# A first layer in plain float32: reordering the lead-in of a chunked attention and mixture-of-experts kernel

## The chip, the cores and the metric

The kernel runs on one core of a Trainium2 chip. The metric is device time in microseconds (us) of one launch. A launch has one program; the inputs are laid out on the host before it (heads split, w1's rows reordered), no arithmetic is done there.

## The reference

Two stages, all float32. Inputs: r, k, v, w of shape (4 batches, 8 heads, 768 positions, 48), u (8, 48), expert weights w1 (4, 384, 1024), w2 (4, 1024, 384) and probabilities for 3072 rows and 4 experts.

```python
for t in range(S):                      # per batch and head, state is 48x48
    cur = einsum('bhd,bhe->bhde', u * k[t], v[t])
    y[t] = einsum('bhd,bhde->bhe', r[t], state + cur)
    state = w[t][..., None] * state + einsum('bhd,bhe->bhde', k[t], v[t])
x = y as rows of 384                    # 8 heads x 48
p = domain_probs / (domain_probs.sum(-1) + 1e-9)
out = sum over e of p[:, e] * (relu(x @ w1[e]) @ w2[e])
```

## The kernel before

**Units and passes.** The 768 positions are cut into 6 chunks of 128; a chunk of one batch is a unit (n = 4 * chunk + batch, 24 units). The experts' part works on blocks; block c is chunk c of all four batches, 512 rows. Passes are pairs of a group of blocks, (0), (1, 2), (3, 4, 5), and an expert; pass 0 is block 0 with expert 0. A turn is one block in one pass: first layer `f1` for 8 tiles of 128 hidden columns, then second layer `f2` per batch. In pass 0 the turn is cut in two half turns of two batches each (`SEG = (2, 2)`), so that the first can start when units 0 and 1 are done.

**Split products.** A float32 matrix is split in a high part (rounded to float32r) and a low part (the rest), and a product is three float32r matmuls: high x high, high x low, low x high. `split_w` makes the parts of a quarter of w1 or w2: one cast on ScalarE, two subtractions of half a tile each on GpSimd (or VectorE). In `f1` a tile takes 9 matmuls (3 slices of the 384 inputs by 3 products), in `f2` 24 per batch. The activation's parts are `hh` (ScalarE) and `hl` (VectorE).

**A unit.** `after_decays` and `until_decays` are scans of the decays on VectorE, `scale` multiplies r and k by them (VectorE), `own_product` and `own_score` make the diagonal term (GpSimd, VectorE's reduction `dg`, then two tiles `a`, one for each head of a pair, from ident on GpSimd or ScalarE), `scores` are plain float32 matmuls of k with r and transposes of k, `masking` copies the scores into `a` (VectorE), `values` multiplies v with `a`, `carry` makes the state. `guard` checks the decays in place (three ScalarE instructions). Four head pairs come out of `values`; x has three slices of 128 rows, each with two heads of 48 rows in rows 0 to 47 and 64 to 111, and the last pair's 96 values are spread over the 2 x 16 rows that are free in each slice. `fill` does that spreading with two DMAs per unit from the tile `y3` (for chunk 0), after ScalarE and VectorE split the values.

**Order.** The order of every engine's work is the order in which the program is written; each engine runs its own instructions in that order, and SP issues all loads in one order too. Up to pass 0 the order is written out by hand (lines 496 to 558). Then `turn` calls `between` after each f1 tile and each quarter of an f2 block (16 calls a half turn), and `gap` adds a pace to a credit and runs one attention step (`go`) per whole credit: `step_a` (after_decays of n+1, scores of n, loads, own_product), `step_b` (until_decays), `step_c` (masking), `step_d` (scale, own_score), `step_e` (values, carry, fill, guard, loads). `work` puts the weight splits in: w2 of a fresh expert in the first half turn, w1 of the next pass in the last second layer. Weights come through a ring `raw` of 4 tiles; `warm_up` issues float32r matmuls on zeros.

Of the kernel before, what the change touches and what calls it, by code (L numbers as in the profile page):

```python
# [20 lines left out]
C = 128  # L21
# [20 lines left out]


@with_exitstack
def chunked_path(ctx, tc, dmaj, tmaj, u_bc, probs, w1, w2, out, flag):
# [35 lines left out]

    def half(j):
        return slice(64 * j, 64 * j + D)
# [26 lines left out]
    def setup_b():  # L110
        nc.gpsimd.memset(mid, -W_MID)
        nc.gpsimd.memset(edge, -W_HALF * W_HALF)
        for t in sd:
            nc.gpsimd.memset(t, 0.0)

# [7 lines left out]
    raw_t, wt = {}, {}  # L123

# [22 lines left out]
    un, xb = {}, {}  # L147
    NU = B * NCH

    def load(n, what):  # L150
# [11 lines left out]
        elif what == "own":  # L162
            if n == 1:

                t = p_acc.tile([128, B, DM], F32, name="acc", tag="acc").rearrange("p b d -> p (b d)")
            else:
                t = p_one.tile([128, 2 * DM], F32, name="rkt", tag="rkt")
            nc.sync.dma_start(out=t[:, 0:2 * DM], in_=tmaj[n, :, 0:2 * DM])
# [11 lines left out]
    def own_score(n):  # L180
# [5 lines left out]
        for q in range(2):  # L186
            a = p_two.tile([128, NP, C], F32, name=f"a{q}", tag=f"a{q}")
            if n <= SEG[0] and q == 1:
# [64 lines left out]
    def values(n):  # L253
        s = un[n]
        c, b, v = s["c"], s["b"], s["v"]

        yp = ps_sc.tile([128, 2, NP, C], F32, name="yp", tag="sc")
        if c == 0:
            y = yp.rearrange("p g (i z) t -> p (g i) z t", z=2)[:, :, 0, :]
        else:  # L260


            y = [yp[:, i % 2, i // 2, :] for i in range(NP)]
            for i in range(NP):
                for j in range(2):
                    o = j ^ (i % 2)
                    nc.tensor.matmul(y[i][wide(o)], sd[n % 2][half(j), i * D:i * D + (64 if o == 0 else D)],  # L267
                                     s["rr"][half(j), i, :], start=(i < 2), stop=False, skip_group_check=True)
        for i in range(NP):
            for j in range(2):  # L270
                h = 2 * i + j
                if c == 0:
                    nc.tensor.matmul(y[wide(j), i, :], v[:, h * D:h * D + (64 if j == 0 else D)],  # L273
                                     s["a"][j][:, i, :], start=(i % 2 == 0), stop=(i % 2 == 1),
                                     skip_group_check=True)
                else:
                    nc.tensor.matmul(y[i][half(j ^ (i % 2))], v[:, h * D:(h + 1) * D], s["a"][j][:, i, :],  # L277
                                     start=False, stop=(i >= 2), skip_group_check=True)
        if c not in xb:
            xb[c] = p_x.tile([128, KT, B, 2, C], F32R, name="x", tag="x")  # L280
        x = xb[c]
        y3 = s["y3"] = p_two.tile([ROWS, 2, 2, C], F32R, name="y3", tag="y3")

        for dst, src in places(s, y if c == 0 else yp):
            nc.scalar.copy(dst[:, :, 0], src)
        for dst, src in places(s, y if c == 0 else yp):
            nc.vector.tensor_tensor(dst[:, :, 1], src, dst[:, :, 0].bitcast(F32), ALU.subtract)

    def places(s, y):
        x, y3 = xb[s["c"]][0:ROWS, :, s["b"]], s["y3"]  # L290
        if s["c"] == 0:
            return (y3[:, 1:2], y[0:ROWS, 3:4]), (x, y[0:ROWS, 0:3])
        return (y3, y[0:ROWS, 1, 0:2]), (x[:, 0::2], y[0:ROWS, 0, 0:2])

    def fill(n):

        s = un[n]
        x, y3 = xb[s["c"]], s["y3"]
        for j in range(2):
            o = 1 - j if s["c"] > 0 else j  # L300
            nc.sync.dma_start(out=x[64 * j + D:64 * (j + 1), :, s["b"]].bitcast(F32),
                              in_=y3[half(o), 1].bitcast(F32))
            if s["c"] > 0:
                nc.sync.dma_start(out=x[half(j), 1, s["b"]].bitcast(F32), in_=y3[half(o), 0].bitcast(F32))
# [39 lines left out]
    def f1(e, blk, f, t0=0, nt=B * C):  # L344
        q, o = divmod(f, FT // NQ)
        wh, wl = wt[e, 1, q]
# [3 lines left out]
        for k in range(KT):  # L350
            for n, (wv, i) in enumerate(((wh, 0), (wh, 1), (wl, 0))):
                nc.tensor.matmul(p[:, 0:nt], wv[:, k, fs], x[:, k, bs, i, :],  # L352
                                 start=(k == 0 and n == 0), stop=(k == KT - 1 and n == 2))
# [80 lines left out]
    steps = [(f, n) for n in range(NU) for f in parts]  # L434
    steps += [(None, NU - 1)] * 8 + [(step_f, NU - 1)]
# [20 lines left out]
    rawq = [(passes[i][1], which, q) for i in fresh for which in (1, 2) for q in range(NQ)]  # L456
# [24 lines left out]
    def turn(e, blk, first, last, b0, nb, work):  # L481
# [3 lines left out]
        def between():  # L485
            work(done[0])
            gap(done[0])
            done[0] += 1

        for f in range(FT):  # L490
            f1(e, blk, f, b0 * C, nb * C)
# [4 lines left out]
    with tc.manual_schedule():  # L496
# [7 lines left out]
        for what in ("w", "k", "r", "own", "v"):  # L504
            load(1, what)
        nc.sync.dma_start(out=pr, in_=probs)
        for q in range(NQ):
            more_raw()
        setup_b()

        decays(0)
        scale(0)
        own_product(0)
        own_score(0)
        after_decays(1)
        scores(0)
        masking(0)
        load(2, "k")
        load(2, "r")
        load(2, "own")  # L520
        guard(0)
        load(2, "w")
        own_product(1)
        until_decays(1)
        scale(1)
        warm_up(FILL[1])
        values(0)
        carry(0)
        fill(0)
        own_score(1)  # L530
        load(2, "v")
        scores(1)
        split_w((0, 1, 0), True)
        masking(1)
        after_decays(2)
        own_product(2)
        warm_up(FILL[2])
        values(1)
        carry(1)
        fill(1)  # L540
        split_w((0, 1, 1), True)
        guard(1)
        setup_c()
        until_decays(2)
        split_w((0, 1, 2), True)
# [230 lines left out]
```

## Time and profile before

| | us |
|---|---|
| median of 3 runs | 930.29 |
| the runs | 930.41, 930.29, 928.63 |
| profiled execution | 928.05 |
| its span, first to last instruction | 926.3 |
| TensorE (PE) busy | 901.4 (97%) |
| VectorE (DVE) / ScalarE (ACT) / GpSimd (POOL) busy | 359.6 / 254.7 / 279.1 |

The chain that ended last is 94% TensorE (44% the second layer, 42% the first layer). PE is the matmuls, PEld the weight loads, SP the engine that issues DMAs; L352 is line 352. "Granted clock" is the share of TensorE's full clock, 1.0 for 2.4 GHz and 0.5 for 1.2 GHz. Busy times of engines overlap, so only TensorE's says something about the span here. The first fortieths of the span are the only ones in which TensorE is not nine tenths busy or more, besides the last.

### The profile page before, as it was taken

Reading aid. Unit: us, or ns where it says so; the run is one execution under the profiler, and the core shown is the slowest. Engines: PE = TensorE matmul, PEld = TensorE weight load, DVE = VectorE, ACT = ScalarE, POOL = GpSimd, SP = SyncE. Lnnn points to the kernel's source line nnn. Section 1 sums busy time; section 2 is a strip of 40 time slices with the busy share of each in tenths; the row PEclk is TensorE's granted clock in tenths of the full one; section 3 lists DMA queues with packets and bytes.
Section 4 is the critical chain, followed back from the end, with each engine's and each line's share of the span. In section 5 each row is a group of like instructions: output and inputs, shape, how many; then the busy total and the mean of one; then the engine's idle time right before and its main releaser. Section 6 shows DMA issues by size and latency. Waiting matters only on the chain.

```text
span 926.3 us, 13725 instructions
## 1 busy us (share of the span) xinstructions
PE 901.4 (97%) x5617; PEld 811.2 (88%) x5617; DVE 359.6 (39%) x567; ACT 254.7 (27%) x462; POOL 279.1 (30%) x283
## 2 busy tenths in 40 slices
PE   7689999999999999999999999999999999999996
PEld 5679889898988989989989898899899899889986
DVE  7756465555454452222455643102222222221221
ACT  3534434313234322231221322232202310321120
POOL 3845667531145414214213220033003300230000
PEclk7789999999999999999999999999999999999999
DMA  8543545432234322102323220022002200111001
GB/s 249 182 129 105 163 149 158 152 105 73 65 115 119 123 72 73 65 1 85 100 81 114 80 79 12 24 69 69 1 1 69 69 1 1 32 37 35 17 18 39
DMA packets 37097, 72.47 MB, mean 78 GB/s; under 512 B 5152, under 2 KB 15648, under 8 KB 37024
## 3 DMA queue, kind: packets, MB, share of 16 engines
q1 hardware_dynamic: 37024, 71.49, 25.2%
q8 instruction: 46, 0.75, 0.3%
q14 instruction: 27, 0.22, 0.1%
HBM read 62.43 MB, written 4.72 MB: 72 GB/s over the span
## 4 chain that ended last, share of the span: by engine, by line
PE 94%; DVE 2%; DMA 2%; ACT 1%; issue 1%; SPq 0%; DVEq 0%
PE pf L372 44%; PE pf L352 42%; PE sc L235 3%; PE yp L277 2%; PE yp L267 1%; PE kt L241 1%; PE up L315 1%; DMA k<-in_dmaj 1%; DMA raw<-in_w 1%; PE yp L273 0%; DVE w2l L142 0%; DMA x<-y 0%; DVE k L227 0%; DVE e L216 0%; PE pf L108 0%
## 5 line engine op out<-in xcount | busy, mean ns | idle before, releaser
L352 PE MATMUL pf<-x,w1h 128*128 128x512 f32 (+1 forms) x1200 | 365.0, 387 | 9.5 <-DMA x<-y 7.0
L352 PEld LDWEIGHTS pf<-x,w1h 128*128 128x128 f32 x1200 | 224.6, 192 | 52.5 <-issue 4.4
L372 PE MATMUL pf<-w2h,hh 128*128 128x384 f32 x768 | 259.3, 338 | 0.0
L372 PE MATMUL pf<-w2h,hl 128*128 128x384 f32 x768 | 257.1, 335 | 0.0
L372 PE MATMUL pf<-w2l,hh 128*128 128x384 f32 x768 | 256.8, 334 | 0.0
L359 DVE SCALAR_TENSOR_TENSOR hl<-pf,hh 128x512 fp32r<-128x512 f32 (+1 forms) x200 | 133.7, 669 | 287.3 <-ACT hh L358 286.9
L358 ACT ACTIVATE hh<-pf 128x512 fp32r<-128x512 f32 (+1 forms) x200 | 116.3, 581 | 448.5 <-PE pf L352 448.4
L352 PE MATMUL pf<-x,w1l 128*128 128x512 f32 (+1 forms) x600 | 231.2, 385 | 0.0
L142 POOL TENSOR_TENSOR w1l<-raw,w1h 128x384 fp32r<-128x384 f32 x80 | 85.1, 1092 | 255.4 <-ACT w1h L137 243.9
L372 PEld LDWEIGHTS pf<-w2h,hh 128*128 128x128 f32 x768 | 144.2, 188 | 2.2 <-issue 0.6
L372 PEld LDWEIGHTS pf<-w2l,hh 128*128 128x128 f32 x768 | 144.2, 188 | 0.8
L372 PEld LDWEIGHTS pf<-w2h,hl 128*128 128x128 f32 x768 | 144.2, 188 | 0.0
L352 PEld LDWEIGHTS pf<-x,w1l 128*128 128x128 f32 x600 | 115.1, 192 | 21.8
L381 DVE SCALAR_TENSOR_TENSOR acc<-pf,pr,acc 128x384 f32<-128x384 f32 x72 | 44.5, 618 | 202.9 <-PE pf L372 202.8
L142 POOL TENSOR_TENSOR w2l<-raw,w2h 128x384 fp32r<-128x384 f32 x78 | 82.6, 1080 | 106.7 <-ACT w2h L137 100.8
L192 POOL TENSOR_TENSOR a<-ident,dg 128x512 f32<-128x512 f32 x45 | 47.7, 1080 | 153.6 <-DVE dg L184 153.6
L235 PEld LDWEIGHTS sc<-r,k 48*128 48x128 f32 x384 | 25.2, 199 | 13.1 <-issue 9.3
L235 PE MATMUL sc<-r,k 48*128 48x128 f32 x384 | 30.0, 299 | 6.2 <-DVE k L227 4.2
L216 DVE TENSOR_TENSOR_SCAN e<-wx,zst 112x516 f32<-112x516 f32 x24 | 34.4, 1433 | 0.8
L251 DVE COPY_PREDICATED a<-mask,sc 128x512 f32<-128x512 uint32 x48 | 32.1, 723 | 3.4 <-POOL a L192 2.1
L379 ACT ACTIVATE acc<-pf,pr 128x384 f32<-128x384 f32 x24 | 14.0, 582 | 70.3 <-PE pf L372 70.2
L204 DVE TENSOR_TENSOR_SCAN g<-wx,ones 112x516 f32<-112x516 f32 x24 | 32.0, 1335 | 2.9 <-DMA wx<-in_dmaj 2.9
(67 smaller groups left out, 436.0 us busy)
## 6 DMA issues: line engine op xcount, KB each, us to landing
raw<-in_w SPq DMA_DIRECT2D x80, 384.0 KB, 3.2
rkt<-in_tmaj SPq DMA_DIRECT2D x23, 384.0 KB, 3.1
wx<-in_dmaj SPq DMA_DIRECT2D x24, 226.2 KB, 3.0
k<-in_dmaj SPq DMA_DIRECT2D x24, 224.0 KB, 3.8
r<-in_dmaj SPq DMA_DIRECT2D x24, 224.0 KB, 3.5
v<-in_tmaj SPq DMA_DIRECT2D x24, 192.0 KB, 2.9
out<-acc SPq DMA_DIRECT2D x24, 192.0 KB, 1.9
x<-y SPq DMA_DIRECT2D x88, 48.0 KB, 2.2
```

The costliest lines, as they stand in the source:

```text
L142: eng.tensor_tensor(lo[:, s], t[:, s], hi[:, s].bitcast(F32), ALU.subtract)
L192: nc.gpsimd.tensor_tensor(a, ident.unsqueeze(1).to_broadcast([128, NP, C]), dg[:, q].unsqueeze(2).to_broadcast([128, NP, C]), ALU.mult)
L204: nc.vector.tensor_tensor_scan(g[:, WLEN - 1:0:-1], wx[:, WLEN - 1:0:-1], ones1[:, WLEN - 1:0:-1], 0.0, ALU.mult, ALU.add)
L216: nc.vector.tensor_tensor_scan(e, wx[:, 0:WLEN - 1], zst.rearrange("p i t -> p (i t)"), 0.0, ALU.mult, ALU.add)
L235: nc.tensor.matmul(sc[:, j, i, :], s["kk"][half(j), i, :], s["rr"][half(j), i, :], start=True, stop=True)
L251: nc.vector.copy_predicated(s["a"][j], mask.unsqueeze(1).to_broadcast([128, NP, C]), s["sc"][:, j])
L277: nc.tensor.matmul(y[i][half(j ^ (i % 2))], v[:, h * D:(h + 1) * D], s["a"][j][:, i, :], start=False, stop=(i >= 2), skip_group_check=True)
L352: nc.tensor.matmul(p[:, 0:nt], wv[:, k, fs], x[:, k, bs, i, :], start=(k == 0 and n == 0), stop=(k == KT - 1 and n == 2))
L358: nc.scalar.activation(hh[:, ts], p[:, 0:nt], AF.Relu)
L359: nc.vector.scalar_tensor_tensor(hl[:, ts], p[:, 0:nt], 0.0, hh[:, ts].bitcast(F32), ALU.max, ALU.subtract)
L372: nc.tensor.matmul(p, hv[:, ts], wv[:, o, :], start=(f == 0 and n == 0), stop=(f == FT - 1 and n == 2))
L381: nc.vector.scalar_tensor_tensor(a[:, b, :], p, sc, a[:, b, :], ALU.mult, ALU.add)
```

## The change

- In pass 0, `f1` multiplies x and w1 in plain float32 (`plain`): 3 matmul calls a tile in place of 9. w1 of expert 0 is loaded unsplit into `w1_own`, which takes one buffer of the x pool, and x unsplit into `x_own`, which takes a buffer of the acc pool. `split_x` makes the float32r parts of x later, in the second layer of pass 0, for the other passes.
- For chunk 0 `values` accumulates all in one tile of the f1 pool: for each of the three slices, two matmuls with the weights `vz`, zeros in 48 of 64 columns and the last pair's v in the other 16 (copied by GpSimd in `last_pair`), and two with v. One ScalarE copy writes x. `fill` does nothing for chunk 0.
- Loads, guards and splits are reordered in the part that is written by hand; unit 1's two diagonal tiles are both made by ScalarE; the fourth warm-up is not called; unit 3's steps go a, c, b, e, d; the first half turn's attention steps are listed in `script`; the pace of the second half turn is (0.2, 0.6).

```diff
FILL = (12, 4, 4, 4)
+DIAG = {0: "pa", 1: "aa", 2: "pa"}
...
     zero = const.tile([128, B * C], F32R, name="zero")
+    vz = [const.tile([128, 2, KT, 64], F32, name=f"vz{i}") for i in range(2)]
...
             nc.gpsimd.memset(t, 0.0)
+        for t in vz:
+            nc.gpsimd.memset(t, 0.0)
...
     raw_t, wt = {}, {}
+    w1_own = p_x.tile([128, NQ, KT * FQ], F32R, name="x", tag="x").bitcast(F32)
+    def load_own(q):
+        nc.sync.dma_start(out=w1_own[:, q], in_=w1[0, q])
...
         wt[key] = (hi.rearrange("p (a f) -> p a f", a=a), lo.rearrange("p (a f) -> p a f", a=a))
-    un, xb = {}, {}
+    un, xb, spare = {}, {}, []
...
             if n == 1:
-                t = p_acc.tile([128, B, DM], F32, name="acc", tag="acc").rearrange("p b d -> p (b d)")
+                spare.append(p_acc.tile([128, B, DM], F32, name="acc", tag="acc").rearrange("p b d -> p (b d)"))
+            if n in (1, 3):
+                t = spare[0][:, (n - 1) * DM:(n + 1) * DM]
...
                 t = p_one.tile([128, 2 * DM], F32, name="rkt", tag="rkt")
-            nc.sync.dma_start(out=t[:, 0:2 * DM], in_=tmaj[n, :, 0:2 * DM])
+            nc.sync.dma_start(out=t, in_=tmaj[n, :, 0:2 * DM])
...
             a = p_two.tile([128, NP, C], F32, name=f"a{q}", tag=f"a{q}")
-            if n <= SEG[0] and q == 1:
+            if DIAG.get(n, "pp")[q] == "a":
...
         c, b, v = s["c"], s["b"], s["v"]
+        if c not in xb:
+            xb[c] = p_x.tile([128, KT, B, 2, C], F32R, name="x", tag="x")
+        x = xb[c]
+        if c == 0:
+            y = ps_f1.tile([128, B * C], F32, name="pf1", tag="pf1")[:, 0:KT * C].rearrange("p (i t) -> p i t", i=KT)
+            z = vz[n % 2]
+            for i in range(KT):
+                for j in range(2):
+                    nc.tensor.matmul(y[64 * j:64 * (j + 1), i, :], z[:, j, i, :], s["a"][j][:, KT, :],
+                                     start=(i == 0), stop=False, skip_group_check=True)
+                for j in range(2):
+                    h = 2 * i + j
+                    nc.tensor.matmul(y[half(j), i, :], v[:, h * D:(h + 1) * D], s["a"][j][:, i, :],
+                                     start=False, stop=(i == KT - 1), skip_group_check=True)
+            nc.scalar.copy(x_own()[:, :, b], y)
+            return
         yp = ps_sc.tile([128, 2, NP, C], F32, name="yp", tag="sc")
...
+    def last_pair(n):
+        v = un[n]["v"][:, 2 * KT * D:].rearrange("p (j g k) -> p j k g", j=2, k=KT)
+        nc.gpsimd.tensor_copy(vz[n % 2][:, :, :, D:], v)
+    def x_own():
+        if len(spare) < 2:
+            spare.append(p_acc.tile([128, B, DM], F32, name="acc", tag="acc").rearrange("p b d -> p (b d)"))
+        return spare[1].rearrange("p (k b t) -> p k b t", k=KT, b=B)
+    def split_x(b):
+        x, t = xb[0][:, :, b], x_own()[:, :, b]
+        nc.scalar.copy(x[:, :, 0], t)
+        nc.vector.tensor_tensor(x[:, :, 1], t, x[:, :, 0].bitcast(F32), ALU.subtract)
+    def fill(n):
+        s = un[n]
         if s["c"] == 0:
+            return
...
-    def f1(e, blk, f, t0=0, nt=B * C):
+    def f1(e, blk, f, t0, nt, plain):
         q, o = divmod(f, FT // NQ)
-        wh, wl = wt[e, 1, q]
...
         p = ps_f1.tile([128, B * C], F32, name="pf1", tag="pf1")
-        for k in range(KT):
-            for n, (wv, i) in enumerate(((wh, 0), (wh, 1), (wl, 0))):
-                nc.tensor.matmul(p[:, 0:nt], wv[:, k, fs], x[:, k, bs, i, :],
-                                 start=(k == 0 and n == 0), stop=(k == KT - 1 and n == 2))
+        if plain:
+            ww = w1_own[:, q].rearrange("p (k f) -> p k f", k=KT)
+            for k in range(KT):
+                nc.tensor.matmul(p[:, 0:nt], ww[:, k, fs], x_own()[:, k, bs, :],
+                                 start=(k == 0), stop=(k == KT - 1))
+        else:
+            wh, wl = wt[e, 1, q]
+            for k in range(KT):
+                for n, (wv, i) in enumerate(((wh, 0), (wh, 1), (wl, 0))):
+                    nc.tensor.matmul(p[:, 0:nt], wv[:, k, fs], x[:, k, bs, i, :],
+                                     start=(k == 0 and n == 0), stop=(k == KT - 1 and n == 2))
...
     steps = [(f, n) for n in range(NU) for f in parts]
+    steps[3 * len(parts):4 * len(parts)] = [(f, 3) for f in (step_a, step_c, step_b, step_e, step_d)]
...
             go()
-    rawq = [(passes[i][1], which, q) for i in fresh for which in (1, 2) for q in range(NQ)]
+    rawq = [(passes[i][1], which, q) for i in fresh for which in (1, 2) for q in range(NQ)][NQ:]
...
             go()
-    def turn(e, blk, first, last, b0, nb, work):
+    def turn(e, blk, first, last, b0, nb, plain, work):
...
         def between():
-            work(done[0])
-            gap(done[0])
+            if not work(done[0]):
+                gap(done[0])
...
         for f in range(FT):
-            f1(e, blk, f, b0 * C, nb * C)
+            f1(e, blk, f, b0 * C, nb * C, plain)
...
         warm_up(FILL[0])
-        for what in ("w", "k", "r", "own", "v"):
+        for what in ("w", "own", "k", "r", "v"):
             load(1, what)
-        nc.sync.dma_start(out=pr, in_=probs)
-        for q in range(NQ):
-            more_raw()
+        load_own(0)
...
         decays(0)
+        guard(0)
...
         own_product(0)
+        last_pair(0)
...
         scores(0)
+        for what in ("w", "k", "r"):
+            load(2, what)
+        load_own(1)
+        load(2, "own")
+        for q in (2, 3):
+            load_own(q)
+        own_product(1)
+        last_pair(1)
+        until_decays(1)
+        guard(1)
+        load(3, "w")
         masking(0)
-        load(2, "k")
-        load(2, "r")
-        load(2, "own")
-        guard(0)
-        load(2, "w")
-        own_product(1)
-        until_decays(1)
-        scale(1)
         warm_up(FILL[1])
+        own_score(1)
...
         carry(0)
-        fill(0)
-        own_score(1)
         load(2, "v")
+        for q in range(2):
+            more_raw()
+        scale(1)
+        after_decays(2)
         scores(1)
-        split_w((0, 1, 0), True)
+        for what in ("k", "r", "own"):
+            load(3, what)
+        for q in range(2):
+            more_raw()
+        nc.sync.dma_start(out=pr, in_=probs)
+        own_product(2)
+        last_pair(2)
+        warm_up(FILL[2])
         masking(1)
-        after_decays(2)
-        own_product(2)
-        warm_up(FILL[2])
+        until_decays(2)
+        guard(2)
+        load(4, "w")
...
         carry(1)
-        fill(1)
-        split_w((0, 1, 1), True)
-        guard(1)
-        setup_c()
-        until_decays(2)
-        split_w((0, 1, 2), True)
-        for what in ("w", "k", "r", "v"):
-            load(3, what)
-        for q in range(3):
-            more_raw()
+        load(3, "v")
         scale(2)
-        own_score(2)
-        load(3, "own")
-        split_w((0, 1, 3), True)
-        owed.append(None)
-        guard(2)
-        load(4, "w")
-        warm_up(FILL[3])
         del un[0], un[1], steps[-2 * len(parts):]
+        script = {0: (lambda: own_score(2),), 1: (go,), 2: (go,), 3: (go,), 4: (go, lambda: last_pair(3)), 5: (go,),
+                  6: (setup_c,), 7: (go,), 8: (go,), 9: (go,), 10: (go, lambda: split_x(0)),
+                  12: (lambda: split_x(1),), 13: (go,)}
...
                     if pi == 0:
-                        pace[:] = (0.625, 0.625) if b0 == 0 else (0.2, 0.4)
+                        pace[:] = 0.2, 0.6
...
                         if own_w2 and i < FT and i % 2 == 0:
-                            split_next((e, 2, q), pi > 0 or q != 1)
+                            split_next((e, 2, q), True)
...
                             read.add(blk)
+                        if pi == 0 and b0 == 0:
+                            for f in script.get(i, ()):
+                                f()
+                            return True
+                        if pi == 0 and i in (9, 11):
+                            split_x(2 + (i - 9) // 2)
...
                         upto(blk * B + b0 + nb - 1)
-                    turn(e, blk, first, last, b0, nb, work)
+                    turn(e, blk, first, last, b0, nb, pi == 0, work)
...
```

## Rows read from the trace of the kernel before

**Rows 1.** Five stretches: busy us (x instructions) by engine, granted clock, DMA share.

```profile
0.00:27.20 27.20, 18.38 (x128) 14.28 (x129) 20.60 (x34) 11.89 (x27) 13.13 (x24) 0.81 0.75 218
27.20:47.70 20.50, 16.15 (x124) 15.05 (x124) 15.94 (x22) 9.77 (x23) 17.46 (x14) 0.75 0.69 217
47.70:63.70 16.00, 11.83 (x104) 11.07 (x101) 10.20 (x17) 6.01 (x14) 10.30 (x9) 0.97 0.47 141
63.70:84.90 21.20, 21.20 (x140) 20.95 (x141) 11.73 (x16) 7.10 (x14) 6.92 (x7) 0.86 0.21 66
84.90:926.30 841.40, 833.80 (x5127) 749.89 (x5125) 301.14 (x481) 219.91 (x385) 231.25 (x231) 1.00 0.23 69
```

**Rows 2.** Chain that ended last, 73 to 95 us: start, length, what.

```profile
73.51 3.25 PE pf L352 x27
76.76 8.32 PE pf L372 x48
...
87.17 0.60 PE yp L267 x12
87.77 1.01 PE yp L277 x16
88.78 0.45 PE up L315 x14
...
93.52 1.09 PE sc L235 x16
94.61 0.53 PE kt L241 x4
```

**Rows 3.** TensorE's waits up to 85 us: total, times, longest.

```profile
PE pf L352 <- DMA x<-y: 7.0, 2, 4.2
PE sc L235 <- DVE k L227: 4.2, 2, 2.3
PE pf L352 <- DVE hl L359: 2.5, 2, 1.6
```

**Rows 4.** Groups by form, 85 to 200 us: total and mean ns; idle before.

```profile
L352 PEld LDWEIGHTS pf<-x,w1h 128*128 128x128 f32 x143 | 26.4, 188 | 5.3
...
L277 PE MATMUL yp<-a,v 128*48 128x128 f32 x96 | 6.5, 277 | 0.0
```

**Rows 5.** Timeline, single rows: start, length, instruction, idle before it.

```profile
5.61 1.23 DVE L216 TENSOR_TENSOR_SCAN e<-wx,zst 112x516 f32<-112x516 f32 x1
...
9.73 1.22 DVE L204 TENSOR_TENSOR_SCAN g<-wx,ones 112x516 f32<-112x516 f32 x1
...
27.21 0.47 PE L352 MATMUL pf<-x,w1h 128*128 128x256 f32 x2 [2.88 <-DMA x<-y]
...
130.64 1.08 PE L277 MATMUL yp<-a,v 128*48 128x128 f32 x16
```

**Rows 6.** Groups by form, 0 to 85 us, GpSimd, VectorE and ScalarE.

```profile
L142 POOL TENSOR_TENSOR w1l<-raw,w1h 128x384 fp32r<-128x384 f32 x14 | 17.1, 1247 | 18.2 <-ACT w1h L137 15.9 <-DMA wx<-in_dmaj 2.3
L216 DVE TENSOR_TENSOR_SCAN e<-wx,zst 112x516 f32<-112x516 f32 x6 | 10.0, 1659 | 0.2
L227 DVE TENSOR_TENSOR k<-k,g 112x512 f32<-112x512 f32 x6 | 9.1, 1516 | 0.0
...
L251 DVE COPY_PREDICATED a<-mask,sc 128x512 f32<-128x512 uint32 x10 | 6.7, 726 | 2.1 <-POOL a L192 2.1
...
L326 ACT ACTIVATE wx<-wx,mid 112x512 f32<-112x512 f32 x5 | 3.7, 735 | 0.0
...
L285 ACT CAST x<-yp 112x384 fp32r<-112x384 f32 x4 | 1.9, 484 | 0.0
```

**Rows 7.** The same view: the low halves that VectorE makes.

```profile
L142 DVE TENSOR_TENSOR w2l<-raw,w2h 128x384 fp32r<-128x384 f32 x2 | 2.3, 1176 | 0.0
```

More of the change, by code (lines that the diff above doesn't have):

```diff
@@ L255, in values @@
         c, b, v = s["c"], s["b"], s["v"]
-        yp = ps_sc.tile([128, 2, NP, C], F32, name="yp", tag="sc")
[L258 to L268, printed above, removed]
+        if c not in xb:
[14 more added lines that the diff above has]
+            return
+        yp = ps_sc.tile([128, 2, NP, C], F32, name="yp", tag="sc")
+        y = [yp[:, i % 2, i // 2, :] for i in range(NP)]
+        for i in range(NP):
+            for j in range(2):
+                o = j ^ (i % 2)
+                nc.tensor.matmul(y[i][wide(o)], sd[n % 2][half(j), i * D:i * D + (64 if o == 0 else D)],
+                                 s["rr"][half(j), i, :], start=(i < 2), stop=False, skip_group_check=True)
         for i in range(NP):
@@ L271, in values @@
                 h = 2 * i + j
[L272 to L278, printed above, removed]
@@ L279, in values @@
-        if c not in xb:
-            xb[c] = p_x.tile([128, KT, B, 2, C], F32R, name="x", tag="x")
-        x = xb[c]
+                nc.tensor.matmul(y[i][half(j ^ (i % 2))], v[:, h * D:(h + 1) * D], s["a"][j][:, i, :],
+                                 start=False, stop=(i >= 2), skip_group_check=True)
         y3 = s["y3"] = p_two.tile([ROWS, 2, 2, C], F32R, name="y3", tag="y3")
-        for dst, src in places(s, y if c == 0 else yp):
+        places = (y3, yp[0:ROWS, 1, 0:2]), (x[0:ROWS, 0::2, b], yp[0:ROWS, 0, 0:2])
@@ L285, in values @@
+        for dst, src in places:
             nc.scalar.copy(dst[:, :, 0], src)
-        for dst, src in places(s, y if c == 0 else yp):
+        for dst, src in places:
             nc.vector.tensor_tensor(dst[:, :, 1], src, dst[:, :, 0].bitcast(F32), ALU.subtract)
[L289 to L293, printed above, removed]
+    def last_pair(n):
+        v = un[n]["v"][:, 2 * KT * D:].rearrange("p (j g k) -> p j k g", j=2, k=KT)
+        nc.gpsimd.tensor_copy(vz[n % 2][:, :, :, D:], v)
@@ L295, in fill @@
+    def x_own():
[6 more added lines that the diff above has]
+        nc.vector.tensor_tensor(x[:, :, 1], t, x[:, :, 0].bitcast(F32), ALU.subtract)
     def fill(n):
         s = un[n]
+        if s["c"] == 0:
+            return
@@ L298, in fill @@
         x, y3 = xb[s["c"]], s["y3"]
         for j in range(2):
-            o = 1 - j if s["c"] > 0 else j
             nc.sync.dma_start(out=x[64 * j + D:64 * (j + 1), :, s["b"]].bitcast(F32),
-                              in_=y3[half(o), 1].bitcast(F32))
-            if s["c"] > 0:
-                nc.sync.dma_start(out=x[half(j), 1, s["b"]].bitcast(F32), in_=y3[half(o), 0].bitcast(F32))
+                              in_=y3[half(1 - j), 1].bitcast(F32))
+            nc.sync.dma_start(out=x[half(j), 1, s["b"]].bitcast(F32), in_=y3[half(1 - j), 0].bitcast(F32))
```

## The prediction

> **What bounds the kernel now.** I read the busy time by stretch first. From 84.9 us to the end TensorE is busy for 833.8 of 841.4 us at full clock, the other engines for 220 to 301 us of it; before 84.9 us it is busy for 18.38 of 27.2, 16.15 of 20.5 and 11.83 of 16.0 us at a mean granted clock of 0.81, 0.75 and 0.97, and the second half turn (63.7 to 84.9) is full but at 0.86 [rows 1]. So what can be won is what TensorE loses before the first pass is over. The chain of waits gives the prices at full clock: 27 first-layer matmuls in 3.25 us, so 0.12 us each and 8.67 for the 72 of a half turn; 48 second-layer ones in 8.32 us; a unit's scores 1.09 and transposes 0.54 us; values, taken as those of line 277, 1.01, and carry 0.45 [rows 2]. Up to 84.9 the useful work is 2 x 8.67 + 2 x 8.32 + 4 x 3.09 (units 0 to 3) + 1.63 (scores of unit 4) = 48.0 us. The other 36.9 us are idle time, half clock and warm-up matmuls. TensorE's waits name the idle part: 7.0 us for the DMAs that place the last head pair in x, 4.2 for VectorE's scaled k, 2.5 for VectorE's hl [rows 3], which stood behind two low halves of w2 on that engine [rows 7].
>
> **The change, part by part.** The state that I compare is "first pass over, unit 4's values and carry done, unit 5's scores done": the new pace (0.2, 0.6) makes 8 x 0.2 + 8 x 0.6 = 6.4, so six, steps in the second half turn. Before gets there, the second pass's own tiles left out, at 84.9 + 0.1 (issue gap) + 0.60 + 1.01 + 0.45 + 1.09 + 0.54 = 88.7 us [rows 2].
>
> *Plain float32 matmuls.* No full-height plain product of this shape stands in the trace. The nearest is the values step: 16 instructions for its 8 float32 products, so two a product; 16 in 1.08 us, of which the last one's own 0.277 is its way through, so (1.08 - 0.28)/15 = 54 ns apart [rows 4, 5]. Each writes half of the array's columns, and taking it that two run side by side, one holds its half for 107 ns with 128 columns. With 256 columns an instruction is 214 ns, or 227 if the 13 ns by which the split product's 120 ns exceeds 256 columns at 2.4 GHz come on top. Bounds for one output tile (3 products, 6 instructions): below, 6 x 0.12 = 0.72, if two did not run side by side and an instruction streamed as fast as a split one [rows 2]; above, 6 x (0.227 + 0.188) = 2.5, if every weight load stood bare [rows 4]. I take 1.33, by the row nearest to it: 10.6 us a half turn in place of 8.67, so +4.0 for both.
>
> *Last pair by TensorE.* values gets 12 products instead of 8: 24 instructions at 63 ns [rows 2], 1.5 instead of 1.0 us, +2.0 for four units. What goes is a pair of DMAs per unit and the split of x ahead of them: the first layer stood idle 2.88 us for these DMAs until 27.21 [rows 5], the second half turn 4.2 [rows 3]. One plain copy on ScalarE (0.48 [rows 6]) is left on the path; the split for the later passes comes in the second layer, where ScalarE and VectorE have room (7.1 and 11.7 of 21.2 us busy [rows 1]): nothing; bare it would be 4 x 1.0. The copies of v and two more memsets on GpSimd fall ahead of its first waited-for product: nothing, or below 1 us bare.
>
> *No split of the first pass's w1.* 8 low halves on GpSimd at 1.25 us and 4 casts on ScalarE go [rows 6]. One w2 low pair moves from VectorE to GpSimd (2.3 us off VectorE [rows 7]): the wait for hl goes. On SP the four loads of w1 now take no ring buffer, hence wait for no split; the loads of unit 2 go between them, and probs goes far back. SP issues in order, so guards 0 and 1 (moved up) and the transposes of unit 0 hold up what stands behind unit 2's wx and k; that is wanted 5 us later at the earliest: nothing. Without that cover a late 384 KB load is about 3 us, the length of the present wait at 27.21.
>
> *The start of the first layer.* VectorE starts the scan of unit 1 at 9.73 as now [rows 5]. Behind it: 1.22, the reverse scan with its two small operations 2.3, masking 0 1.45, a reduction 0.54: 15.2. TensorE waits for masking 0 (14.7), then values 0 (1.5, or 2.8 at half clock), carry 0.5, scores 1 (1.1 to 2.1): 17.8 to 20.1; VectorE scales unit 1 and scans unit 2 beside that. Then masking 1 1.45, reverse scan of unit 2 2.2, guard 2 on ScalarE (two activations of 0.735 and a read: 1.65), which is queued ahead of the copy of x, and the copy 0.48 [rows 6]: 23.6 to 25.9. I take 24.6, 2.6 us ahead of 27.21.
>
> *First half turn.* TensorE's work: 8 tiles 10.6, scores and transposes of units 2 and 3 3.3, their values and carry 3.9, two blocks of second layer 8.3: 26.1, so 50.7. What is late next is VectorE, in its written order: hl 0, reduction of unit 2, hl 1 (its hh stands behind four activations of the new diagonal on ScalarE: about 29.3), scan 3, hl 2, reverse scan 3 (2.4), hl 3, masking 2: 35.7. TensorE has six tiles and scores 2 done at 24.6 + 8.0 + 1.65 = 34.2 and waits 1.5 us. Then hl 4, scaling 3 (up to 2.4 beside GpSimd), a reduction, hl 5 at 39.4: tile 7 gets its buffer 0.3 late. Masking 3 (behind setup_c and scan 4, at 45.8) is 0.35 late. GpSimd has from 27.2 on 13 operations at 1.25 [rows 6] (8 low halves, three diagonals, unit 3's own product): 43.5, and the last low half is wanted at 45.5. So 2.2 us of waits; bounds are 0 and, if VectorE's list in this stretch is half as long again, 6.
>
> *Clock.* After 2.88 us of idle TensorE the stretch from 27.2 shows 0.75, after 4.2 us that from 63.7 shows 0.86 [rows 1, 3, 5]: 3.0 us lost in the second (0.14 x 21.2). Here about 2 us of idle stand ahead of the first layer and none between the half turns. I put 1.0 on it, between 0 and the 3.0.
>
> *Second half turn.* x is there before the second layer ends: 10.6 + 8.3 + scores 4 1.6 + values and carry 4 with their gaps 2.7 + scores 5 1.6 = 24.9.
>
> **The sum.** 50.7 + 2.2 + 1.0 + 24.9 = 78.8 against 88.7: 9.9 us less. The profiled execution took 928.05 (span 926.3), which gives 918.1. It stands 2.2 us under the median of the runs, 930.29; with half of that offset added I predict 919.
>
> The Trainium skill has a rule that speaks against this: TensorE: Matmul & The Clock Gate, Part 3 (The mechanism), says that a weight load overlaps matmuls in flight only where its row group differs from theirs. By it every full-height product would stand behind its load, and the time would be that of the first rival. The trace does not agree for the split products: 188 ns a load, yet 0.12 us a product, load and all [rows 2, 4]; for plain float32 at full height no row shows it.
>
> **Rivals.**
> *Bare weight loads* (the other side): each of the 96 first-layer instructions of the pass waits for its own 128-column load, 0.188 us [rows 4], 18.0 us more: 919 + 18 = 937, slower. It decides from 9.9/96 = 0.10 us of bare load an instruction. For it: no row has this shape; against it: the split products hide theirs in 0.12 us. 0.05.
> *VectorE as the bound:* the scans and scalings run as the slow ones do all through the first half turn (the reverse scan took 1.66 on average up to 85 us, 1.23 with GpSimd idle; the scaled k 1.52 [rows 5, 6]), masking 2 and 3 come 1 to 2 us later still, and the clock stretch costs its whole 3.0: gain 3 to 7, so 921 to 926. For it: VectorE's list there is as long as TensorE's. Against: GpSimd is freed of 10 us ahead of it. 0.19.
> *Nothing late:* the first layer starts at 23.6, no waits, full clock: 4.2 us more gain, 913 to 916. For it: TensorE has hardly an idle stretch behind 15 us by the sum. 0.15.
> *No net effect:* the start is no earlier than 27, a w2 half comes 3 us late, and the 6.0 us of added TensorE work eat the rest: within 2 us of before. 0.06, a third of it slower.
>
> **How the numbers follow.** The forecast (gain 7 to 13, 916 to 922) has 0.55, the rivals 0.05, 0.19, 0.15 and 0.06. From 912 to 925 lie the forecast and nearly all of the second and third rival: 0.85. A difference of 0.2% (1.9 us) is what a measurement can tell from none. Faster: 0.55 + 0.19 + 0.15, less 0.01 for their ends, 0.88; within 0.2%: 0.05; slower: 0.07.
>
> **What would show it.** In the changed kernel's profile: tiles of the first pass with 6 instructions 214 to 227 ns apart at full clock (near 400 with bare loads, 120 if they stream like split ones); the first of them at 23.6 to 25.9; no wait of TensorE for a DMA on x, and the second half turn straight behind the second layer; what waits there are, for VectorE's masking and hl, 2 to 3 us in all; the second pass's first tile about 6 us earlier than now (78.8 against 84.9), with unit 4's values and unit 5's scores already behind it. A start of the first layer after 27 us would be wrong, and so would a gain or loss that arises after the first pass.

## The result and the profile after

The changed kernel takes 916.79 us (median of 4 runs, 915.55 to 917.89), the kernel before, run beside it, 930.35 (4 runs, 928.63 to 930.83): a ratio of 0.9857 [0.9838, 0.9877]. The forecast was 919.0, the range 912 to 925. The profiled execution took 917.89 (span 916.0), 10.16 less than the profiled one of before; the medians differ by 13.6, because before's profiled execution (928.05) was quicker than any of its 4 runs here.

Busy time by stretch, cut where the forecast had its steps, as in [rows 1]: the stretch and its length; busy us of PE, PEld, DVE, ACT and POOL, with instruction counts in brackets; granted clock, DMA share, GB/s moved.

```profile
0.00:24.60 24.60, 17.94 (x140) 14.39 (x140) 18.98 (x29) 10.57 (x25) 10.67 (x24) 0.79 0.95 273
24.60:50.70 26.10, 23.60 (x187) 19.86 (x188) 20.30 (x30) 12.18 (x30) 18.97 (x18) 0.93 0.66 191
50.70:78.80 28.10, 28.10 (x198) 25.73 (x200) 16.28 (x29) 13.66 (x31) 11.38 (x11) 1.00 0.24 71
78.80:916.00 837.20, 831.06 (x5077) 748.17 (x5075) 301.62 (x476) 217.69 (x380) 232.80 (x231) 1.00 0.23 70
```

From 50.7 us on TensorE has no gap left before the second pass and runs at full clock; before, it idled 4.2 us of the stretch 47.7 to 63.7 and ran the next at 0.86. Its waits up to 80 us, as in [rows 3] (total, times, longest):

```profile
PE pf L278 <- DVE a L264: 3.6, 4, 2.7
PE pf L381 <- ACT acc L284: 2.3, 1, 2.3
PE sc L248 <- DVE k L240: 1.7, 1, 1.7
PE pf L112 <- POOL zero L94: 1.4, 1, 1.4
```

No line names a DMA or hl any more. In their place stand the masking (L264), and the copy of x (L284) ahead of the first layer. The chain that ended last, as in [rows 2] (start, length, what), from the masking of unit 1 to the second pass; L381 is the plain first-layer matmul, L387 the split one (L407, further below, is the second layer):

```profile
20.42 1.36 DVE a L264 x2
21.79 0.75 DVE zst L227
...
22.77 1.24 DVE e L229
24.04 0.73 ACT wx L355
24.80 0.81 ACT wx L356 x2
25.61 0.37 ACT acc L284
26.03 4.54 PE pf L381 x12
...
37.03 1.34 DVE a L264 x2
...
56.01 6.47 PE pf L381 x30
...
80.24 4.84 PE pf L387 x21
```

The start of the first layer hangs, as the forecast had it, on masking 1, the reverse scan (L229), the guard on ScalarE (L355, L356) and the copy. Its first 12 instructions took 4.54 us, the 30 of the second half turn 6.47: 378 ns an instruction at a granted clock of 0.61 (26.0 to 30.4 us, so partly at either level), against 216 at 1.00. The second pass's first tile stands at 80.24, where the state compared with (units 4 and 5 done) needed 88.7 before.

### The profile page after: what moved, and what is told of

The parts are those of the page before. It is cut to its first block, busy times and chain, and to the rows that moved or that the text cites. A ratio compares the mean times of both kernels' runs of the same rounds, so it can differ in the third digit from the quotient of the medians.

```text
span 916.0 us, 13636 instructions
## 1 busy us (share of the span) xinstructions
PE 900.7 (98%) x5597; PEld 808.2 (88%) x5597; DVE 357.2 (39%) x561; ACT 254.1 (28%) x462; POOL 273.8 (30%) x282
## 4 chain that ended last, share of the span: by engine, by line
PE 96%; DVE 1%; DMA 1%; issue 0%; ACT 0%; SPq 0%; DVEq 0%
PE pf L407 44%; PE pf L387 41%; PE sc L248 3%; PE yp L298 2%; PE pf L381 2%; PE yp L293 1%; PE kt L254 1%; PE up L344 1%; DMA wx<-in_dmaj 1%; DVE a L264 1%; PE pf L278 0%; DVE g L217 0%; PE pf L282 0%; DVE zst L227 0%; DVE e L229 0%
## 5 line engine op out<-in xcount | busy, mean ns | idle before, releaser
L387 PE MATMUL pf<-x,w1h 128*128 128x512 f32 x1104 | 342.1, 391 | 0.0
L407 PE MATMUL pf<-w2h,hh 128*128 128x384 f32 x768 | 259.6, 338 | 0.0
L407 PE MATMUL pf<-w2h,hl 128*128 128x384 f32 x768 | 257.1, 335 | 0.0
L407 PE MATMUL pf<-w2l,hh 128*128 128x384 f32 x768 | 256.8, 334 | 0.0
L387 PEld LDWEIGHTS pf<-x,w1h 128*128 128x128 f32 x1104 | 205.8, 188 | 42.5 <-issue 0.4
L387 PE MATMUL pf<-x,w1l 128*128 128x512 f32 x552 | 215.2, 390 | 0.0
L153 POOL TENSOR_TENSOR w1l<-raw,w1h 128x384 fp32r<-128x384 f32 x72 | 74.8, 1068 | 254.6 <-ACT w1h L148 254.6
L407 PEld LDWEIGHTS pf<-w2h,hh 128*128 128x128 f32 x768 | 144.2, 188 | 2.2 <-issue 0.4
L407 PEld LDWEIGHTS pf<-w2l,hh 128*128 128x128 f32 x768 | 144.2, 188 | 0.9
L407 PEld LDWEIGHTS pf<-w2h,hl 128*128 128x128 f32 x768 | 144.2, 188 | 0.0
L387 PEld LDWEIGHTS pf<-x,w1l 128*128 128x128 f32 x552 | 103.6, 188 | 21.8
L153 POOL TENSOR_TENSOR w2l<-raw,w2h 128x384 fp32r<-128x384 f32 x80 | 85.1, 1085 | 110.9 <-ACT w2h L148 101.4
L264 DVE COPY_PREDICATED a<-mask,sc 128x512 f32<-128x512 uint32 x48 | 32.2, 722 | 3.0 <-PE sc L248 3.0
L229 DVE TENSOR_TENSOR_SCAN e<-wx,zst 112x516 f32<-112x516 f32 x24 | 32.9, 1372 | 0.8
L148 ACT CAST w2h<-raw 128x768 fp32r<-128x768 f32 x40 | 33.1, 826 | 0.0
L304 ACT CAST y<-yp 112x256 fp32r<-112x256 f32 x20 | 7.5, 373 | 89.5 <-PE yp L298 88.4
```

What stands on the lines that cost most here:

```text
L148: nc.scalar.copy(hi, t)
L153: eng.tensor_tensor(lo[:, s], t[:, s], hi[:, s].bitcast(F32), ALU.subtract)
L229: nc.vector.tensor_tensor_scan(e, wx[:, 0:WLEN - 1], zst.rearrange("p i t -> p (i t)"), 0.0, ALU.mult, ALU.add)
L264: nc.vector.copy_predicated(s["a"][j], mask.unsqueeze(1).to_broadcast([128, NP, C]), s["sc"][:, j])
L407: nc.tensor.matmul(p, hv[:, ts], wv[:, o, :], start=(f == 0 and n == 0), stop=(f == FT - 1 and n == 2))
```

## Experiments

Times are medians in us; a ratio is that to the kernel before. The kernels were timed in three groups, each on one chip beside runs of the kernel before:

| group | kernel before | runs |
|---|---|---|
| 1 | 928.85 | the changed kernel once more, guard later, masking earlier, both |
| 2 | 928.09 | split parts back, pair alone, pair by DMAs, warm-up |
| 3 | 928.29 | DMAs with w2 later, odd tiles, all three, old pace |

"The change" below is the repeat's 917.71; across groups the ratios are the better comparison.

**The changed kernel once more.** Nothing is edited.

> The changed kernel once more, unaltered, for its spread beside the kernels it is compared with. The profiled executions differ by 10.2 us (928.05 and 917.89), the medians by 13.6, and the changed kernel's four runs reach from 915.55 to 917.89 with granted clocks from 0.997 down to 0.991. Theory: the 2.3 us between its runs are half-clock time of TensorE in the first 31 us, so a slower run has a lower mean clock. Rival: they lie at the end of the program, where the profiled execution of before spent 7.6 us behind its last matmul and this one 6.1. Median expected: 916 to 918.

917.71 (5 runs, 916.24 to 920.02), 0.988 [0.9856, 0.9905]. The profiled execution, 916.24, is 1.65 us shorter than the first one, of the same program. Its chain:

```profile
19.82 1.36 DVE a L264 x2
21.19 0.17 DVE zst L227
...
24.84 2.86 PE pf L381 x12
...
34.87 1.34 DVE a L264 x2
...
53.84 6.47 PE pf L381 x30
...
78.07 4.16 PE pf L387 x18
```

Two stretches show the greater part of why, in the first execution and, below it, in this one; the granted clock is the third number from the end:

```profile
9.90:20.30 10.40, 7.73 (x64) 6.27 (x63) 8.12 (x10) 6.44 (x18) 5.10 (x4) 0.53 1.05 293
...
26.00:30.40 4.40, 4.37 (x12) 3.38 (x12) 0.89 (x2) 1.75 (x5) 0.61 (x1) 0.61 1.04 310
```

```profile
9.90:20.30 10.40, 8.08 (x71) 6.87 (x70) 8.42 (x11) 6.44 (x19) 5.92 (x6) 0.74 1.05 316
...
26.00:30.40 4.40, 4.40 (x34) 3.66 (x34) 1.93 (x4) 3.18 (x8) 2.77 (x3) 1.00 1.02 323
```

In the repeat the first 12 instructions of the first layer take 2.86 us instead of 4.54, and it starts 1.2 us earlier. Of this 1.2, 0.6 are there at masking 1, in part by the clock of the first stretch (the scores of unit 1 took 1.18 us instead of 1.52); the other 0.6 is the small VectorE operation L227, 0.17 us here and 0.75 in the first chain (see the last section). So the 2.2 us at the second pass's first tile belong to one execution, most of them to its clock, not to the kernel; whether both ran on one chip is not on record. The rival, the end of the program, goes the other way: the first execution has 6.1 us behind its last matmul, the repeat 6.7. The runs' times go roughly with their mean clock (916.24 at 0.995, 917.71 at 0.994, 918.62 at 0.991, 920.02 at 0.992), as before's do (926.45 at 0.990, 932.91 at 0.978).

**Split weights and split x put back into the first layer.** The last pair by TensorE and most of the new order are kept; w1 comes through the ring again, so the loads of w2 now stand between and behind its splits (the edit is cut to its main lines).

```diff
@@ fill phase @@
+        split_x(0)
...
+        split_w((0, 1, 0), True)
...
+        for q in range(1, NQ):
+            split_w((0, 1, q), True)
+            more_raw()
...
-                    turn(e, blk, first, last, b0, nb, pi == 0, work)
+                    turn(e, blk, first, last, b0, nb, False, work)
```

> The changed kernel with the first layer of its first turn as three float32r products again: w1 split as in the kernel before, each unit's x split right behind its values; the rest of the new order stays, the last pair by TensorE too. Theory (GpSimd's and ScalarE's splits cost more in the lead-in than TensorE's 4.0 us of plain products): the 8 low halves put 10 us more ahead of the diagonal of unit 2 and of w2's low halves on GpSimd, TensorE waits for masking 2 and for w2; 1 to 6 us above the changed kernel. Rival (TensorE's own work bounds the turn, splits are hidden): 4 us below it.

923.47, 0.9947 [0.9932, 0.9961]: about 6 us slower than the change, though TensorE needs some 3.4 us less for the first layer of the pass (an estimate: 96 plain instructions at 216 ns are 20.7 us, against 2 x 8.67). GpSimd's timeline, which the chain that ended last goes through, names the reason, split weights first, changed kernel second (start, length, line, operation, tile):

```profile
31.34 6.27 POOL L151 TENSOR_TENSOR w1l<-raw,w1h 128x384 fp32r<-128x384 f32 x6
37.58 2.89 POOL L151 TENSOR_TENSOR w2l<-raw,w2h 128x384 fp32r<-128x384 f32 x2
40.43 1.96 POOL L203 TENSOR_TENSOR a<-ident,dg 128x512 f32<-128x512 f32 x1
```

```profile
31.70 1.05 POOL L205 TENSOR_TENSOR a<-ident,dg 128x512 f32<-128x512 f32 x1
```

The diagonal of unit 2 queues behind eight low halves and ends 9.6 us later; the masking, which writes into the same tile, cannot end before 43.8 (38.4 in the first execution of the change, 36.2 in the repeat). From 26 to 60 us TensorE waits 3.1 us for maskings; in the first half turn of the change it was 1.0 and 1.7:

```profile
PE pf L276 <- DVE a L262: 3.1, 2, 2.8
```

Scores 1 are late too, at 22.36 against 18.81, in part because VectorE's share of the split of x stands ahead of the scaling of unit 1; but masking 2 comes later still, and by it GpSimd's queue decides. So plain float32 pays by the work that it takes off the other engines, GpSimd above all, not on TensorE, where it costs.

**The last head pair by TensorE, alone, in the kernel before.**

```diff
+    vz = [const.tile([128, 2, KT, 64], F32, name=f"vz{i}") for i in range(2)]
...
+        if c == 0:
...
+                    nc.tensor.matmul(y[64 * j:64 * (j + 1), i, :], z[:, j, i, :], s["a"][j][:, KT, :],
+                                     start=(i == 0), stop=False, skip_group_check=True)
...
+            nc.scalar.copy(x[:, :, 0], y)
+            nc.vector.tensor_tensor(x[:, :, 1], y, x[:, :, 0].bitcast(F32), ALU.subtract)
+            return
```

> The kernel before with this one part of the change: values of chunk 0 with the last pair placed by TensorE, x split from it, no DMAs. First theory: of the 7.0 us of waits for these DMAs only the second (4.2 us, with 3.0 us of half clock behind it) goes, as the first layer's start at 24.9 instead of 27.2 is followed by the wait for VectorE's scaled k, which comes at 32.0 as before; less 2.0 us of products: 4 to 6 us below before. Rival (waits add up): 8 to 9 us below. Second rival (the hand order gives all): 0 to 2.

923.45, 0.9947 [0.9932, 0.9961]: 4.6 us faster, as the first theory had it. Against [rows 3], the 7.0 us for the DMAs on x are gone, but the wait for scaled k grew from 4.2 to 6.8 and the one for hl from 2.5 to 3.0:

```profile
PE sc L239 <- DVE k L231: 6.8, 3, 4.2
PE pf L379 <- DVE hl L386: 3.0, 2, 1.8
```

The kernel with split weights, which has the pair and the new order, takes as long as this one: without the plain matmuls the order, as far as that run kept it, adds nothing.

**The change with the last pair moved by DMAs again.**

```diff
+            y3 = s["y3"] = p_two.tile([ROWS, 2, 2, C], F32R, name="y3", tag="y3")
+            nc.scalar.copy(y3[:, 0, 0].bitcast(F32), y[0:ROWS, KT])
+            nc.scalar.copy(x_own()[0:ROWS, :, b], y[0:ROWS, 0:KT])
...
+            for j in range(2):
+                nc.sync.dma_start(out=x_own()[64 * j + D:64 * (j + 1), :, s["b"]],
+                                  in_=s["y3"][half(j), 0, 0].bitcast(F32))
```

> The changed kernel with the last head pair of chunk 0 placed by two DMAs a unit again (8 products a unit, a copy of that pair on ScalarE, plain float32 as in the changed kernel). Theory: the first layer starts 2.5 to 3 us later, as it waits for the DMAs of unit 1, with half clock more likely behind the idle time; those of unit 3 fall into the second layer's last 5 us and cost nothing; 4 x 0.5 us of products come back: 1 to 3 us above the changed kernel. Rival (the DMAs are hidden, the products are not): 2 us below it.

926.58 (12 runs), 0.9983 [0.9974, 0.9993]: about 9 us slower than the change, where 1 to 3 were expected. TensorE's wait and the chain into it:

```profile
PE pf L380 <- DMA acc<-y: 11.9, 1, 11.9
```

```profile
20.40 0.42 SPq L138
...
20.88 6.10 DMA raw<-in_w
...
27.04 0.57 SPq L325
...
27.66 5.72 DMA acc<-y
...
33.58 4.99 PE pf L380 x12
```

The chain puts a load of w2 ahead of the pair's DMA in SP's queue (issued at 27.04), and the pair's two DMAs, of 24 KB each, then need 5.72 us to land beside 384 KB loads.

**The same with the four loads of w2 behind the fill of unit 1.**

```diff
@@ against the kernel with DMAs @@
-        for q in range(2):
-            more_raw()
...
-        for q in range(2):
-            more_raw()
...
+        for q in range(4):
+            more_raw()
```

> The kernel with the two DMAs a unit again (dma_back), but the four loads of w2 are issued behind unit 1's DMAs instead of ahead of them. There TensorE waited 11.9 us for these DMAs. Theory (they stood in line: SP issues in order and took them up at 27.0, and they landed 5.7 us later behind the w2 loads): the wait falls to 3 to 6 us and the time by 4 to 7 us against dma_back, unless the later w2 then holds up the first half turn by 1 to 3. Rival (the DMAs of 16 rows by 3 x 128 elements are slow by themselves): no change.

921.68, 0.9921 [0.99, 0.9942]: 4.9 us of it come back by the medians, 5.8 by the ratios. The pair now lands in 2.12 us, and the first layer starts at 29.61:

```profile
27.35 2.12 DMA acc<-y
...
29.61 4.93 PE pf L380 x12
```

So somewhat more than half of the 9 us lay in the neighbourhood of the w2 loads. Of what is left, 2.9 us are the DMA step on the path, from the end of ScalarE's copies (26.71) to the first matmul, and about 2 the lower clock of the 12 instructions behind it (4.93 us against 2.86).

**Guard 2 behind the values of unit 1.** ScalarE does two activations of 0.73 to 0.81 us for it ahead of the copy of x.

```diff
-        guard(2)
-        load(4, "w")
         values(1)
         carry(1)
         load(3, "v")
         scale(2)
+        guard(2)
+        load(4, "w")
```

> Guard 2 and the load behind it are written after the values and the scaling of unit 2, so the copy of unit 1's x on ScalarE no longer waits for guard 2 (24.04 to 25.61). Theory (a chain into the first layer, then TensorE's own work): the first layer starts at 24.0 to 24.4 instead of 26.03, and the result is 1.5 to 2.5 us below the changed kernel's, as less idle time also makes a half-clock stretch less likely. Rival (VectorE's list bounds the first half turn): hl 5 and masking 2 come when they came, the gain is under 0.5 us.

913.95 (913.55 to 914.87), 0.9835 [0.9811, 0.9858]: 3.8 us below the changed kernel's 917.71 on the same chip, no run of the one within those of the other. By the profiled spans (911.9 against 914.4) it is 2.5, of which 2.0 stand in the lead-in (the second pass's first tile at 76.11 against 78.07), within the 1.5 to 2.5 expected. The wait for the copy fell to 0.2 us, from 1.7 in the repeat, and the first layer starts at full clock:

```profile
23.82 2.86 PE L381 MATMUL pf<-acc,x 128*128 128x256 f32 x12 [0.21 <-ACT acc L284]
```

**Masking of unit 2 one step earlier.** In the order of steps, masking stands ahead of the scan of the unit behind it.

```diff
+    steps[2 * len(parts):3 * len(parts)] = [(f, 2) for f in (step_a, step_c, step_b, step_d, step_e)]
```

> Unit 2's steps go a, c, b, d, e: masking 2 is written ahead of the reverse scan of unit 3. Theory (the wait of TensorE for masking 2 is what the first half turn loses): values 2 start 1.2 us earlier and the result is 1.0 to 1.5 us lower. Rival (VectorE's whole list is the bound): the buffer for tile 7 waits for hl 5, which stands behind the same list and comes at 41.9 as now; what the one wait gives back the other takes, 0 to 0.3 us.

915.57 (914.72 to 915.99), 0.9848 [0.9824, 0.9872]: 2.1 below the changed kernel's median, 0.7 by the profiled spans (913.6 against 914.4). In its profile the first layer starts at 25.86, 1.0 later than in the repeat, for reasons that lie ahead of the edit: the reverse scan of unit 2 took 1.89 us beside a GpSimd addition, 1.23 in the repeat. So the worth of the step is not settled.

**Both together.**

```diff
+    steps[2 * len(parts):3 * len(parts)] = [(f, 2) for f in (step_a, step_c, step_b, step_d, step_e)]
...
-        guard(2)
-        load(4, "w")
...
+        guard(2)
+        load(4, "w")
```

> Both edits. Chain theory: the sum of the two, 2.5 to 4 us below the changed kernel. VectorE as the bound: what the later guard gives alone, at most 2 us, with a wait for hl 5 in the trace in place of that for masking 2.

914.48 (912.51 to 914.87), 0.9833 [0.9809, 0.9857]: no more than the guard alone. Masking 3 becomes what TensorE follows, and it stands at the end of a row of VectorE's work:

```profile
40.12 0.41 DVE hl L394
40.53 1.90 DVE g L217
42.42 1.25 DVE a L264 x2
```

**Guard later, and the splits of w2 behind the odd tiles.**

```diff
-                        if own_w2 and i < FT and i % 2 == 0:
+                        if own_w2 and i < FT and i % 2 == (1 if pi == 0 else 0):
```

> guard_later, with the four splits of w2 in the first half turn behind tiles 1, 3, 5, 7 in place of 0, 2, 4, 6. In guard_later ScalarE's cast of the first w2 quarter waited for its load until 26.57 with hh 1 and unit 2's diagonal behind it. Theory (this queue position is what the first half turn now waits for): masking 2 comes 1.5 to 2.5 us earlier, the result is 1 to 2 us below guard_later. Rival (VectorE's list is the bound): below 0.5 us.

913.37 (912.37 to 917.01), 0.9841 [0.9815, 0.9867], 0.6 below guard later alone by the medians and nothing by the ratios (0.9841 and 0.9835). Masking 2 began at 32.80, against 33.64 with the guard alone. So ScalarE's casts held up that stretch by less than 1 us, and the rival, VectorE's list, fits better.

**All three, with setup_c behind masking 3.**

```diff
-                  6: (setup_c,), 7: (go,), 8: (go,), 9: (go,), 10: (go, lambda: split_x(0)),
+                  7: (go,), 8: (go, setup_c), 9: (go,), 10: (go, lambda: split_x(0)),
```

> guard_later with masking 2 first, w2 split behind odd tiles, and the sum of the probabilities moved behind masking 3 (VectorE spends 1.5 to 2.5 us on it ahead of masking 3). If VectorE's list is the bound in the first half turn, masking 3 comes 1.5 to 2 us earlier than in both (42.4) and the result is 1.5 to 3 us below guard_later; if TensorE's own work is the bound by now, the same within 1 us.

913.71 (913.23 to 914.9), 0.9836 [0.9814, 0.9858]. Between 20 and 60 us TensorE waits 0.7 us in all, so that TensorE's own work bounds that stretch, as the second expectation had it; GpSimd's low halves are most of what is left:

```profile
PE pf L407 <- POOL w2l L153: 0.5, 2, 0.3
```

The four versions with a later guard (913.37 to 914.48) are not told apart. The simplest, guard later alone, beats both kernels.

**Eight warm-up matmuls ahead of the first layer.**

```diff
         carry(1)
+        warm_up(8)
```

> The changed kernel with 8 more warm-up matmuls behind carry 1, in the 2.3 us in which TensorE waits for unit 1's x. Theory (part of the time and of the spread between runs is half clock in the first layer, due to that idle stretch): no half-clock stretch behind 20 us, the slow runs go, the median is 0.5 to 2 us lower. Rival (the clock is not what differs): the same time within 0.3 us, or later by up to 1 us where the 8 matmuls outlast the wait.

916.92 (4 runs, 916.4 to 917.77), 0.988 [0.9862, 0.9898], the repeat's ratio. The idle time ahead of the first layer is filled, and it runs at full clock:

```profile
24.14 2.04 PE pf L112 x8
26.18 2.59 PE pf L381 x12
```

The stretch 9.9 to 20.3 still has 0.53 there. The runs lie closer together than the repeat's, but no gain of the median is shown. The copy that the first layer needs is done at 25.71, so the eight matmuls outlast the wait by some 0.4 us; whether the fill costs as much as it saves stays open.

**The old pace in place of the script by hand.**

```diff
-        script = {0: (lambda: own_score(2),), 1: (go,), 2: (go,), ...
+        own_score(2)
+        setup_c()
...
-                        pace[:] = 0.2, 0.6
+                        pace[:] = (0.625, 0.625) if b0 == 0 else (0.2, 0.4)
```

> The changed kernel with the first half turn's attention steps given out by the old pace (0.625 a gap, units' steps in the order a to e) in place of the list by hand, own_score 2 and the sum of the probabilities ahead of the half turn as before, old pace in the second half turn too. Theory (what counts is the lead-in and what engines are freed of, the list only moves waits): masking 2 waits less, values 3 come at the end of the second layer and delay the second half turn by about 1 us; 0 to 2 us above the changed kernel. Rival (the list by hand is a main part of the gain): 4 us or more above it.

920.1, 0.9915 [0.9893, 0.9936]: 2.4 above the repeat's median, 3.2 by the ratios, between the two theories; the intervals of the ratios overlap. Part of it is this edit's own: the sum of the probabilities now stands ahead of hl on VectorE, and waits for a load:

```profile
24.52 8.06 DMA pr<-in_probs
...
33.69 0.35 DVE hl L394
34.08 8.31 PE pf L381 x30
```

What the script by itself is worth is not settled.

## Why the prediction held, step by step

The mechanism was right: a good part of what TensorE lost before the end of the first pass went. Its idle time there fell from 17.3 us up to 84.9 to 9.2 up to 78.8, by [rows 1] and the table of stretches above. One statement failed: 1.3 to 1.8 us of the gain arose behind the first pass, which the forecast had ruled out (see below). And luck helped the number: in the first execution the lead-in came 1.4 us later than forecast and the rest 1.8 earlier, so that 917.89 stands beside 918.1. The 0.9 that was added for the median went the wrong way, as the first execution is 1.1 slower than the median of its runs. By its terms, in the first execution and in the repeat:

| step | forecast | first | repeat |
|---|---|---|---|
| first layer starts | 24.6 | 26.03 | 24.84 |
| masking 2 is done | 35.7 | 38.37 | 36.21 |
| second half turn starts | 53.9 | 56.01 | 53.84 |
| second half turn lasts | 24.9 | 24.2 | 24.2 |
| second pass's first tile | 78.8 | 80.24 | 78.07 |
| execution | 918.1 | 917.89 | 916.24 |

- *Plain matmuls.* Forecast 214 to 227 ns an instruction, 216 measured (6.47/30). A tile is 1.29 us instead of 1.33. By the rule of the Trainium skill (TensorE: Matmul & The Clock Gate, Part 3, The mechanism) that a weight load overlaps matmuls only where its row group differs, each would have stood behind its load of 188 to 202 ns. The trace does not agree: the 30 instructions leave no room for a load between them. The rival of bare loads is refuted.
- *The start* came just behind the half-clock end of its bounds in the first execution (26.03 against 25.9) and near the value taken in the repeat. The list of instructions was complete. Masking 1 came past and near the late end of its bounds (20.42 and 19.82 against 17.8 to 20.1), by the clock of values 0 and scores 1; from there to the first layer both were shorter than the 5.8 forecast (5.6 and 5.0), the repeat by the quick L227.
- *Last pair by TensorE.* Values and carry of unit 2 run from 38.51 to 40.36 in the first execution: 1.85 us, against 1.5 + 0.5.
- *The clock* was put behind the start, at 1.0 us. It cost 1.7 there in the first execution (4.54 against the repeat's 2.86 us) and nothing in the repeat, and up to 0.6 more ahead of it. It is a spread between executions, not a term.
- *Waits in the first half turn.* Forecast 2.2 us; TensorE waited 1.0 and 1.7 us for maskings (L264) there. VectorE was next, as said, but never ran up the 6 us of the bound; the rival that made it the bound priced it too high. With the guard out of the way it is what ends last, as the run with both edits showed.
- *DMAs.* No wait named one, so the cover held. Its price without cover, "about 3 us" for a late 384 KB load, no run tested. The run with the pair on DMAs shows another thing: the new order of SP's loads, with those of w2 so early, makes the pair's DMAs dearer (11.9 us of waiting) than they had been in the kernel before (7.0 in two waits). The sum did not need that number.
- *Behind the pass* the forecast had 837.6 us left; 835.8 and 836.3 were measured. Of the first one's 1.8 us, 1.4 lie behind the last group of second-layer matmuls, which ends 7.6 us ahead of the span's end before and 6.1 after (6.7 in the repeat); before first, after second:

```profile
902.04 16.68 PE pf L372 x96
```

```profile
893.19 16.68 PE pf L407 x96
```

  No edit of the change reaches there, yet it is no chance of one execution: this tail is 7.5 to 7.8 us in the profiles of before, split parts back, pair alone and the two kernels with DMAs, and 6.1 to 6.7 in the nine others. In the five there are five packets of the instruction queue (q14) behind the last VectorE operation, in the nine four. So the tail goes with the program as it is loaded; the cause is not shown. About 1 us of what split parts back and the kernels with DMAs are slower than the change lies there.
- *The parts.* The pair alone gave 4.6 us, the rest without the pair about 1.5 (926.58 against 928.09), all of it 11 to 14. That looks as if they did not add, but the 1.5 hold the price of the pair's DMAs among the w2 loads. With these loads later the rest without the pair gave 6.6 (921.68 against 928.29), and 4.6 and 6.6 make 11.2, near the repeat's 11.1: by these two runs they do add.

## What to carry to other kernels

Price an edit on a full engine by what it frees on the others: the plain matmuls cost TensorE 3.4 us and still brought 6, because GpSimd's queue was what the masking waited for. Removing one wait can lengthen the next, as the pair alone showed; sum the path after the edit, not the waits before it. And profile the same program twice before reading 1 or 2 us out of one trace.

## What was not expected of the hardware

A small DMA behind big ones is dear: two of 24 KB took 5.72 us to land among 384 KB loads, 2.12 with these issued behind them.

A tiny VectorE operation can take as long as what is left of a GpSimd operation on large tiles. The 112x4 operation of L227 took 0.84 us at 21.68 in the first execution and 0.27 at 21.08 in the repeat, and both times it ended 0.02 to 0.04 us behind the GpSimd addition in which it began. First execution, then repeat:

```profile
21.50 1.00 POOL L191 TENSOR_TENSOR rkt<-rkt,u_sb 128x384 f32<-128x384 f32 x1
```

```profile
21.68 0.84 DVE L227 TENSOR_SCALAR zst<-g 112x4 f32<-112x4 f32 x1
```

```profile
20.30 1.01 POOL L191 TENSOR_TENSOR rkt<-rkt,u_sb 128x384 f32<-128x384 f32 x1
```

```profile
21.08 0.27 DVE L227 TENSOR_SCALAR zst<-g 112x4 f32<-112x4 f32 x1
```

With GpSimd idle, as in the run with warm-ups, it took 0.15.
